# A planned two-layer kernel: one more resident value slice, smaller attention buffers, a new order and a new pacing of transfers

## Chip, cores and metric

The kernel runs on one core of one Trainium2 chip. The metric is the device time of one execution in microseconds (us); the times shown are the median of three runs.

## What is computed

The input x has 2048 tokens of 640 numbers in bfloat16. Two kinds of layer follow each other, twice each with the same weights: x = x + A(layernorm(x)), x = x + B(layernorm(x)).

Layer A is attention over segments of 32 tokens with a recurrent memory of 8 rows. It has 32 heads of 192. For each of 64 segments, in order:

```python
h = jnp.concatenate([mem, xs], axis=1)               # 40 rows
q, k, v = h @ Wq, h @ Wk, h @ Wv                     # 640 -> 32 heads x 192 each
p = softmax(where(mask, q @ k.T * scale, -1e9))
o = (p @ v) @ Wo                                     # 6144 -> 640
mem = o[:, :8, :]; outs.append(o[:, 8:, :])
```

The memory rows of a segment's output are the memory of the next segment, so the segments are a chain. Layer B is an MLP mixer: layer norm, a 640x640 matmul and a tanh-GELU, a shift of four feature groups by one or two tokens, a second 640x640 matmul, then a block 640 to 1536 to 640 with a GELU.

## The kernel before

Both attention layers run at once, in two lanes. Lane 1 is the second layer and runs LAG = 5 segments behind lane 0. `attention_step(t)` does segment t of lane 0 and segment t - 5 of lane 1 side by side, in the columns of one tile `hT`, so that one pass of the weights through TensorE serves both. There are 69 steps: 0 to 4 have only lane 0, 5 to 63 both, 64 to 68 only lane 1. With two lanes a matmul's moving operand has 80 columns (40 rows a lane), with one lane 56.

In a step the 32 heads are 8 groups of four (`HG = 4`), and two groups make a pair. For each of the four pairs, `keys_queries` projects keys and queries of a group (L940), `values3` (two lanes, L993) or `values` (one lane, L1028) the values of the pair, and `attend` does scores (`pss`, L1048), masked softmax on VectorE and ScalarE (L1060 to L1073, into the tile `Pm` or, in even two-lane steps, `Pm_e`), transposes (`pst`, L1082, copied into `PT` at L1090), the weighted values (`pso`, L1099) and their copy into an `oT` buffer (L1110, L1112). `project` multiplies oT by the output weights and accumulates all groups in `psy` (L1134). L1161 copies the new memory rows from `psy` into the next step's `hT`: nothing of the next step's projections can start before that. In even two-lane steps some value rows of the next step are computed ahead and put by in `stash`, and fetched back in the odd step (L1011).

`WO_FROM` says from which group on a projection may be held to the end of the step; it keeps its oT buffer until then, and `OT_BUFS` is their number. The MLP runs in chunks of 64 tokens a lane, one chunk for every two steps, from an even step on (`chunk`, `chunk_end`: psx, psl, psv2, psh, hs, y), between the attention's matmuls.

The attention weights are 31.5 MB [...]. `STREAM` says for each kind and pair how many of the five 128-row slices are loaded anew in every step; the other slices stay. A slice of a pair is 128x1536 bfloat16, 384 KB, and goes into one of 12 ring slots (`wst`, L817). Odd steps go through the pairs backwards, so that the pair at a turn is loaded once for two steps. The output weights are resident (L801). The MLP's weights pass through three slots (`wstB`, L853 to L859). All these loads are issued by SP in one order.

The order of all work is planned when the program is built. `Plan.add` records each operation with its engine, an estimate of its duration, what it reads and writes, a due time and a rank from the table `RANK`. `Plan.place` is a list scheduler: it always places the operation that can start first, and ranks decide among those that can start at nearly the same time. It models transfers with a rate (`DMA_RATE`, with one lane `RATE_ONE`). A load that would put more than 1 us of work ahead in the transfer model is delayed, and is "paced": in the program it waits for a matmul group, which the last lines of the kernel choose:

```python
elif o.paced:
    k = len(done) - 1
    while k >= 0 and done[k].end + PE_LAT > o.start:
        k -= 1
    if k >= 0:
        tc.add_manual_dep(o.last, done[k].last.name, dep, reason="pace")
```

Of the kernel before, what the change touches and what calls it, by code (L numbers as in the profile page):

```python
# [21 lines left out]
HG = 4  # L22
STREAM = {"k": (4, 2, 2, 4), "q": (4, 2, 2, 4), "v": (4, 1, 2, 4)}
# [8 lines left out]
WO_FROM = 3  # L32
# [9 lines left out]
OT_BUFS = 5  # L42
# [5 lines left out]
SWITCH = 0.095  # L48
LAT = 0.12
PE_LAT = 0.3  # L50
DMA_RATE = 350.0e3
# [9 lines left out]
RATE_ONE = 360.0e3  # L61
# [6 lines left out]
        "apply_ln.f": (29.559, 55.792, 17.416,),  # L68
        "chunk.f1": (23.781,),
        "chunk.f2": (55.346,),  # L70
        "chunk.f3": (49.334,),
        "chunk.fe": (36.823,),
        "chunk.fe3": (102.823,),
        "chunk.fel": (55.768,),
        "chunk.fh": (108.157,),
        "chunk.fhr": (14.733,),
        "chunk.fhs": (-1.703,),
        "chunk.fl": (17.93,),
        "chunk.fs": (3.514, 106.703,),
        "chunk.ft": (21.572,),  # L80
        "chunk.ftl": (23.993,),
        "chunk.fw": (19.421, 33.626, 37.652, 47.067, 46.903, 46.908, 51.102, 31.274, 56.07, 81.64, 83.785, 53.43,
            79.164,),
        "chunk.fx": (15.161,),
        "chunk.fx0": (112.491, 68.494,),
        "chunk.fxu": (105.007,),
        "chunk.fz": (124.455,),
        "gelu.f1": (41.515, 31.842, 65.448, 69.413, 29.704, 45.171, 6.969,),
        "gelu.f2": (19.582, 55.401, -1.038, -13.207, 27.337, 61.156, 95.68,),
        "gelu.f3": (36.826, 58.297, 18.949, 4.948, 30.821, 34.558, 18.885,),  # L90
        "gelu.f4": (55.18, 34.768, 63.375, -56.037, -0.096, 18.35, 22.907,),
        "ln_ops.f1": (3.817, 60.955,),
        "ln_ops.f2": (114.827, 95.473,),
        "load_b.fn": (42.665, 72.601, 73.122, 60.79, 46.44, 71.473, 46.173, 41.023, -13.973, -19.336, 68.295,
            43.387, 34.395,),
        "transposes.f": (18.738, 60.298, 22.802,),
    },
    "chunk_end": {
        "apply_ln.f": (40.67,),
        "chunk_end.fc": (62.442, 58.834, 83.754,),  # L100
        "chunk_end.fs": (36.579, 19.311,),
        "chunk_end.fst": (24.833, 137.421,),
        "chunk_end.fw": (77.354, 82.175, 46.044, 93.892, 86.198, 104.308,),
        "chunk_loads.f": (110.369, 92.579, 122.005, 106.334, 106.331,),
        "chunk_loads.fz": (111.9, -5.695,),
        "ln_ops.f1": (7.196,),
        "ln_ops.f2": (123.331,),
        "load_b.fn": (5.23, 1.719, 91.203, 49.097, 74.715, 52.663,),
        "transposes.f": (106.447,),
    },  # L110
    "first": {
        "attention_step.attend.f1": (68.897, 39.326, 41.804, 28.466, -8.574, 3.827, 12.182, 81.811,),
        "attention_step.attend.f2": (29.688, 3.725, 55.817, 85.348, 89.532, 54.11, 46.47, 42.088,),
        "attention_step.attend.f3": (37.804, 74.562, 24.632, 39.11, 84.711, 2.334, 12.184, 31.815,),
        "attention_step.attend.f4": (46.985, 133.184, 57.996, -14.888, 44.577, 61.056, 25.057, 28.659,),
        "attention_step.attend.f5": (72.24, 28.209, 80.373, 49.346, -18.442, -28.685, 28.798, 35.564,),
        "attention_step.attend.f6": (7.921, 29.359, -30.003, 43.173, 18.344, 41.846, 42.511, 55.051,),
        "attention_step.attend.f7": (13.361, 7.383, 43.256, 25.908, 20.236, 55.857, 75.302, -11.96, 21.812, -5.753,
            19.773, 72.6, 75.299, 95.674, 86.699, 88.497,),
        "attention_step.attend.fs": (46.721, 6.105, 1.413, -7.834, 21.699, 20.254, 21.569, 46.62,),  # L120
        "attention_step.fm": (55.427,),
        "attention_step.fy": (-0.204,),
        "attention_step.keys_queries.fk": (26.488, 18.209, 58.728, 7.772, 36.409, 64.332, -3.077, 23.72,),
        "attention_step.keys_queries.fk2": (-14.703, 2.672, 48.256, 53.233, 34.025, 40.988, 45.598, -2.059, 1.962,
            15.275, 34.847, -10.142, 39.767, 56.809, 63.46, 66.992,),
        "attention_step.keys_queries.fn": (21.571, 32.111, 16.117, -56.342, -41.907, 1.871, 54.408, 55.614, 11.212,
            18.753, 53.715, 66.651, 18.167, 23.251, 31.271, 32.948, 29.756, 7.549, 39.591, 50.473, -0.315, 18.167,
            48.365, 58.168, 44.747, 139.641, 21.246, 32.364, 22.87, 41.262, 64.464, 48.46, 83.925, 17.007, 19.065,
            16.202, 18.756, 33.666, 34.528, 40.661, 38.815, 44.173, 28.507, 19.545, 33.472, 24.726, 15.715, 51.317,
            45.935, 22.944, -5.271, 29.206, 49.555, 26.526, 25.7, 16.824, 43.548, 57.875, 33.742, 59.147, 64.063,  # L130
            27.622, 29.175, 81.7,),
        "attention_step.keys_queries.fq": (45.809, 18.135, 60.1, 65.753, 69.37, -1.427, 49.622, 44.462,),
        "attention_step.project.f8": (19.52, 33.909, -28.707, 107.592, 12.86, 77.771, 100.466, 23.989, 31.803,
            40.827, 40.837, 130.729, 36.057, 48.362, 41.26, 49.706,),
        "attention_step.v_copy.fe": (42.261, 47.784, 48.887, 71.528, 12.202, 49.386, 41.804, 50.823, 64.266,
            49.318, 20.738, 66.436, 42.958, 63.832, 23.717, 24.613,),
        "attention_step.values.fv": (-41.285, 32.943, 26.797, 50.039, 35.587, 16.299, 43.359, 44.868,),
        "load_pair.fn": (14.648, 53.698, 35.518, 22.343, -20.956, 37.306, 71.774, 39.237, 19.839, 12.575, 20.573,
            58.077, 54.069, 54.009, 75.338, 62.619, 8.153, -3.245, 80.829, 54.072, 43.384, 63.592, 35.638, 18.998,
            20.67, 44.7, 62.346, 9.067, 39.164, 19.703, 48.316, 36.251, 10.435, 5.137, 75.941,),  # L140
        "res_tile.fn": (73.432, 28.558, 56.529, 20.582, 69.248, 38.979, 29.597, 74.898, 15.641, 75.959, 55.693,
            44.577, 0.319, 29.095, 42.3, 49.248, 29.964, 107.836, 49.865, 17.493,),
    },
    "last": {
        "apply_ln.f": (-20.574, 76.742, 91.655,),
        "chunk.fc2": (45.814, 9.139,),
        "chunk.fhr": (-49.46,),
        "chunk.fs": (65.9, 36.918,),
        "chunk.ft": (54.865,),
        "chunk.fw": (48.117, 33.495, 45.73, 17.024, 46.488, 12.234, 41.248, 25.194, 32.675, 94.494, 70.8,),  # L150
        "chunk.fx": (25.434,),
        "chunk.fxu": (45.171,),
        "chunk.fz0": (78.323,),
        "chunk.halves.fa": (27.094, 106.57,),
        "chunk.halves.fd": (-49.02, 71.767,),
        "chunk.halves.fn": (77.02,),
        "gelu.f1": (17.472, 32.155, 99.763, 91.572, 38.995, 48.095,),
        "gelu.f2": (11.863, 37.133, 19.592, 31.791, 91.583, 13.808,),
        "gelu.f3": (38.816, 63.043, 83.342, 80.205, 21.478, 58.951,),
        "gelu.f4": (-10.272, 39.611, -4.107, 48.457, 78.558, 99.684,),  # L160
        "ln_ops.f1": (28.421, -18.981,),
        "ln_ops.f2": (44.289, 103.361,),
        "load_b.fn": (21.293, 70.515, 34.095, 6.385, 49.625, 62.984, 43.433, 10.52, 22.43, 49.618, 76.588, 9.262,
            76.276,),
        "transposes.f": (31.423, -1.2,),
        "warm.fwarm": (32.401, -16.818, 47.675, 21.047, 64.891, 28.29, 48.878, 42.379, 30.258, 92.789, 28.894,
            39.585, 19.172,),
    },
    "last_end": {
        "chunk_end.fs": (103.409, 12.202,),  # L170
        "chunk_end.fst": (53.517, 65.451, 1.877, 30.054,),
        "chunk_end.fw": (48.61, 122.515, 29.136, 50.074, 10.083, 12.93, 28.51, 21.247,),
        "load_b.fn": (11.244, 75.885, 68.713, 49.999, 55.019, 53.695,),
    },
    "start": {
        "apply_ln.f": (103.828,),
        "chunk_loads.f": (0.033, 14.73, 144.506,),
        "ln_ops.f1": (24.785,),
        "ln_ops.f2": (122.216,),
        "start.f1": (65.561,),  # L180
        "start.f2": (79.115,),
        "start.f3": (47.921,),
        "start.f4": (33.718,),
        "start.f5": (40.419, 48.193, 69.503, 117.792,),
        "transposes.f": (62.646,),
    },
    "step0": {
        "attention_step.attend.f1": (-11.22, 35.238, 17.075, 18.583, 70.388, 34.765, 47.388, 68.986,),
# [1571 lines left out]
```

## Time and profile before

| | |
|---|---|
| median of three runs | 3275.02 us (3273.39 to 3279.2) |
| the profiled execution, its own time | 3273.35 us |
| its span, first to last instruction | 3271.6 us |
| mean granted TensorE clock | 0.992 |
| moved by DMA | 860.41 MB, mean 263 GB/s |
| matmuls, and as many weight loads | 77341 |

In the profile, PE is TensorE's matmuls and PEld its weight loads, DVE is VectorE, ACT ScalarE, POOL GpSimd, and SP issues transfers. L940 is line 940 of the kernel before. A matmul's end is modelled: its recorded duration is some 0.2 us, while matmuls of 80 columns start 36 ns apart. "Idle before" an instruction is time after the modelled end of the one before it, with the releaser that ended the wait; "issue" means that no releaser is known. Numbers in waits are total us, times, and the longest in us.

### The profile page before, as it was taken

How to read it: one execution, taken by the hardware profiler on the slowest of the kernel's cores; microseconds unless marked ns; L12 is line 12 of the kernel's file. 1: busy time of each engine (PE TensorE's matmuls, PEld its weight loads, DVE VectorE, ACT ScalarE, POOL GpSimd, SP SyncE). 2: the span in 40 equal slices, each digit the busy share in tenths (PEclk: the TensorE clock that was granted, in tenths of full speed). 3: DMA queues.
4: the chain of work that ended last, by engine and by line, in shares of the span. 5: the costliest groups of instructions: out<-in, count | busy, mean ns of one | idle time of the engine just before them, and what ended most of it. 6: DMA issues, size and time to landing. Idle time of an engine off the chain costs nothing.

```text
span 3271.6 us, 173713 instructions
## 1 busy us (share of the span) xinstructions
PE 3154.7 (96%) x77341; PEld 2792.5 (85%) x77341; DVE 2314.6 (71%) x6857; ACT 1891.5 (58%) x4837; POOL 242.1 (7%) x485
## 2 busy tenths in 40 slices
PE   6899999999999999999999999999999999999987
PEld 4778888888888888888888888888888888888776
DVE  3566777777777777777777777777777777777665
ACT  2346566666565666665656666565656666656443
POOL 0000000000000000000000000000000000000000
PEclk7999999999999999999999999999999999999999
DMA  9887778777777877787778777877877787778786
GB/s 374 280 283 261 247 257 273 248 247 270 269 255 249 278 258 248 248 284 262 255 243 289 246 242 253 278 253 242 278 260 248 248 282 260 256 242 289 266 280 221
DMA packets 419560, 860.41 MB, mean 263 GB/s; under 512 B 40784, under 2 KB 208415, under 8 KB 418808
## 3 DMA queue, kind: packets, MB, share of 16 engines
q1 hardware_dynamic: 411512, 836.21, 74.6%
q8 instruction: 606, 9.93, 1.2%
q0 software_dynamic: 7136, 13.00, 1.2%
q14 instruction: 146, 1.20, 0.1%
q10 hardware_dynamic: 160, 0.08, 0.0%
HBM read 843.88 MB, written 5.24 MB: 260 GB/s over the span
## 4 chain that ended last, share of the span: by engine, by line
PE 90%; DMA 4%; DVE 2%; issue 2%; ACT 1%; SPq 0%; POOL 0%; POOLq 0%; ACTq 0%; DVEq 0%
PE psy L1134 17%; PE psq L940 17%; PE psk L940 17%; PE psv L993 15%; PE pss L1048 5%; PE pso L1099 4%; PE y L1599 3%; PE psh L1553 3%; PE pst L1082 2%; DMA wst<-in_A_Wq_dram 2%; PE psv L1028 2%; PE psh L1431 1%; PE hs L1490 1%; DMA wst<-in_A_Wk_dram 1%; PE psv L1204 1%
## 5 line engine op out<-in xcount | busy, mean ns | idle before, releaser
L940 PEld LDWEIGHTS <-wst 128*128 128x128 bf16 x19872 | 803.8, 99 | 64.4 <-issue 47.2
L1134 PE MATMUL psy<-oT,wo 128*128 128x80 bf16 (+1 forms) x16560 | 697.6, 200 | 24.9 <-issue 11.7
L973 ACT CAST V<-psv 96x384 bf16<-96x384 f32 (+4 forms) x1264 | 588.8, 473 | 213.1 <-PE psv L993 140.7
L1134 PEld LDWEIGHTS <-wo 128*128 128x128 bf16 x16560 | 628.0, 99 | 68.2 <-issue 53.8
L940 PE MATMUL psq<-hT,wst 128*128 128x80 bf16 (+1 forms) x9936 | 543.8, 200 | 25.6 <-DVE hT L1161 14.9
L940 PE MATMUL psk<-hT,wst 128*128 128x80 bf16 (+1 forms) x9936 | 533.9, 200 | 7.5 <-issue 4.6
L993 PEld LDWEIGHTS <-hT 128*32 128x32 bf16 (+1 forms) x11840 | 294.8, 96 | 162.5 <-issue 9.1
L948 ACT CAST qT<-psq 128x480 bf16<-128x480 f32 (+1 forms) x552 | 291.4, 528 | 136.8 <-PE psq L940 108.0
L993 PE MATMUL psv<-wst,hT 128*32 128x384 bf16 x6512 | 366.4, 326 | 0.0
L1060 DVE CUSTOM_DVE_ANT_1 pss<-pss,mask 80x320 f32<-80x320 f32 (+2 forms) x552 | 258.3, 468 | 127.8 <-PE pss L1048 84.0
L963 ACT CAST kT<-psk 64x160 bf16<-64x160 f32 (+1 forms) x552 | 152.0, 275 | 323.4 <-PE psk L940 134.0
L940 PE MATMUL psq<-hT,wq 128*128 128x80 bf16 (+1 forms) x6624 | 320.1, 200 | 7.2 <-issue 3.5
L940 PE MATMUL psk<-hT,wk 128*128 128x80 bf16 (+1 forms) x6624 | 321.4, 200 | 2.2 <-issue 1.2
L993 PE MATMUL psv<-wv,hT 128*32 128x384 bf16 x5328 | 321.6, 328 | 0.2 <-issue 0.2
L1110 ACT CAST oT<-pso 128x240 bf16<-128x240 f32 (+1 forms) x552 | 189.0, 342 | 227.2 <-PE pso L1099 172.4
L1112 DVE CAST oT<-pso 128x240 bf16<-128x240 f32 (+1 forms) x552 | 213.4, 387 | 127.4 <-ACT oT L1110 59.7
L963 DVE CAST kT<-psk 64x160 bf16<-64x160 f32 (+1 forms) x552 | 174.2, 316 | 181.6 <-ACT kT L963 129.2
L1090 ACT COPY PT<-pst 80x320 bf16<-80x320 bf16 (+2 forms) x552 | 220.9, 400 | 131.6 <-PE pst L1082 123.1
L956 DVE CAST kT<-psk 128x320 bf16<-128x320 f32 (+1 forms) x552 | 255.8, 463 | 45.0 <-ACT kT L963 31.4
L940 PEld LDWEIGHTS <-wk 128*128 128x128 bf16 x6624 | 268.1, 100 | 13.0 <-issue 12.7
L940 PEld LDWEIGHTS <-wq 128*128 128x128 bf16 x6624 | 266.2, 99 | 9.3 <-issue 5.5
L1048 PE MATMUL pss<-kT,qT 128*128 128x80 bf16 (+2 forms) x3312 | 242.8, 210 | 13.9 <-issue 3.8
(148 smaller groups left out, 4265.1 us busy)
## 6 DMA issues: line engine op xcount, KB each, us to landing
wst<-in_A_Wk_dram SPq DMA_DIRECT2D x556, 384.0 KB, 5.0
wst<-in_A_Wq_dram SPq DMA_DIRECT2D x556, 384.0 KB, 5.0
wst<-in_A_Wv_dram SPq DMA_DIRECT2D x487, 384.0 KB, 5.2
wstB<-in_B_w_dram SPq DMA_DIRECT2D x495, 320.0 KB, 4.8
wstB<-in_B_w_dram SPq DMA_DIRECT2D x132, 160.0 KB, 4.4
wo<-in_A_Wo_dram SPq DMA_DIRECT2D x8, 960.0 KB, 12.3
xw<-in_A_x_dram POOLq DMA_DIRECT2D x31, 80.0 KB, 4.8
x2d<-vbg POOLq DMA_DIRECT2D x31, 80.0 KB, 5.1
```

The costliest lines, as they stand in the source:

```text
L940: nc.tensor.matmul(out=o[:, cc, 0:W], lhsT=wv(kc, GW * j + cc * P, GW * j + (cc + 1) * P), rhs=h[:, kc, cw:cw + W], start=begin(pq), stop= ...
L948: nc.scalar.copy(out=qT[:, :, c0:c0 + N], in_=T(pq)[:, :, off:off + N])
L956: nc.vector.tensor_copy(out=k4[:, :, 0::3, c0:c0 + N], in_=p4[:, :, 0::2, off:off + N])
L963: copy(out=k4[r0:r1, :, jj, c0:c0 + N], in_=p4[r0:r1, :, 1, off:off + N])
L973: (nc.vector.tensor_copy if e == "DVE" else nc.scalar.copy)(out=v_part(*dst), in_=a_)
L993: nc.tensor.matmul(out=o[32 * u:32 * u + n3, :], lhsT=left[:, kc, 32 * g3:32 * g3 + n3], rhs=wv(kc, a, a + GWH), start=(kc == 0), stop=(kc ...
L1048: nc.tensor.matmul(out=o[0:m_, i * N:(i + w_) * N].rearrange("p (a b) -> p a b", a=w_), lhsT=qTw[:, c * NS:c * NS + m_], rhs=k_[:, j:j + w ...
L1060: nc.vector.tensor_tensor_reduce(out=o, in0=o, in1=maskt.unsqueeze(1).to_broadcast([NR, HG, N]), scale=-scale, scalar=3.0e38, op0=ALU.add, ...
L1090: nc.scalar.copy(out=Pt[0:KV, :, 0:N], in_=T(pst)[0:KV, :, c0:c0 + N])
L1110: nc.scalar.copy(out=o_[:, 3:6, off:off + N], in_=T(pso)[:, 3:6, 0:N])
L1112: nc.vector.tensor_copy(out=o_[:, 0:3, off:off + N], in_=T(pso)[:, 0:3, 0:N])
L1134: nc.tensor.matmul(out=o[:, m, cw:cw + W], lhsT=wo[:, cc, m * P:(m + 1) * P], rhs=o_[:, cc, 0:W], start=st, stop=True, skip_group_check=True)
```

## The change

One more of the five value slices of pair 2 stays on chip. Room for it, 3072 bytes in each partition, comes from three oT buffers instead of five, from one softmax tile `Pm` with the wider layout for all steps instead of two tiles, and from a `stash` without its gaps, whose copies are then two instructions in place of one. Projections of groups 3 and 4 are no longer held to the end. A load is tied to a matmul group that may end up to 0.25 us later than before; the planner's rates are lower and some of its estimates differ. Key and query projections get order edges (each starts after the first part of the one before; the second group of a pair with two lanes waits for the values of the pair before), one-lane values come after the scores planned before them and leave one PSUM slot free, and the whole table of ranks is another.

```diff
-STREAM = {"k": (4, 2, 2, 4), "q": (4, 2, 2, 4), "v": (4, 1, 2, 4)}
+STREAM = {"k": (4, 2, 2, 4), "q": (4, 2, 2, 4), "v": (4, 1, 1, 4)}
-WO_FROM = 3
+WO_FROM = 5
-OT_BUFS = 5
+OT_BUFS = 3
-SWITCH = 0.095
+SWITCH = 0.105
 LAT = 0.12
+PACE = 0.25
+OVER = 0.07
-DMA_RATE = 350.0e3
+DMA_RATE = 335.0e3
-RATE_ONE = 360.0e3
+RATE_ONE = 350.0e3
 RANK = {
...
-            free[e] = o.end
+            free[e] = o.end - (OVER if e in ("ACT", "DVE") else 0.0)
...
-    stash = ctile([P, 2, 2 * VP], bf16, "stash")
-    Pmw = ctile([NS, HG * NS], bf16, "Pm")
-    Pm = Pmw[:].rearrange("p (c n) -> p c n", c=HG)
-    Pm_e = ctile([NS, (HG - 1) * KR + P], bf16, "Pm_e")
+    stash = ctile([P, 2, 2, 2 * Dh], bf16, "stash")
+    Pmw = ctile([NS, (HG - 1) * KR + P], bf16, "Pm")
+    Pm = Pmw[:, 0:HG * KR].rearrange("p (c n) -> p c n", c=HG)[:, :, 16:KR]
...
+    last_v = []
+    seq_kq = []
...
-                    last_op[kind] = add("PE", mm_us(W, k=GC * len(kcs)), due + 0.01 * kcs[0], fn, r=(wb, *hk), a=(pq,))
+                    last_op[kind] = add("PE", mm_us(W, k=GC * len(kcs)), due + 0.01 * kcs[0], fn, r=(wb, *hk), a=(pq,),
+                                        order=(*(last_v[-2:-1] if j and both else ()), *seq_kq[-1:]))
+                    own_kq.append(last_op[kind])
+                seq_kq.append(own_kq[0])
...
                 def fst(op, j=j):
-                    st_, v_ = stash[32 * pr:32 * pr + 32, j, :], Vt[j][64:96, :] if behind_v else Vt[j][0:32, :]
-                    nc.vector.tensor_copy(out=v_ if behind_v else st_, in_=st_ if behind_v else v_)
+                    rows = Vt[j][64:96, :] if behind_v else Vt[j][0:32, :]
+                    for a in range(2):
+                        st_ = stash[32 * pr:32 * pr + 32, j, a, :].rearrange("n (h e) -> n h e", h=2)
+                        v_ = rows.rearrange("n (h x) -> n h x", h=2)[:, :, 256 * a:256 * a + Dh]
+                        nc.vector.tensor_copy(out=v_ if behind_v else st_, in_=st_ if behind_v else v_)
...
-                pv = ps("A", [P, GWH], f32, "psv")
+                pv = ps("A", [P, GWH], f32, "psv", 1)
...
-                add("PE", mm_us(GWH, k=KC), s0 + 0.05 * hf * sl, fv, r=(*wbs, *hk), w=(pv,), mode=64)
+                add("PE", mm_us(GWH, k=KC), s0 + 0.05 * hf * sl, fv, r=(*wbs, *hk), w=(pv,), mode=64, order=placed_before("pss"))
...
-            while k >= 0 and done[k].end + PE_LAT > o.start:
+            while k >= 0 and done[k].end + PE_LAT > o.start + PACE:
                 k -= 1
```

## Prediction before the run

> **What bounds the kernel now.** I read engine shares first, then the run cut into stages, then TensorE's waits by stage, then transfers. From the page:
>
> ```profile
> PE 3154.7 (96%) x77341; PEld 2792.5 (85%) x77341; DVE 2314.6 (71%) x6857; ACT 1891.5 (58%) x4837; POOL 242.1 (7%) x485
> ```
>
> TensorE is the bound; the question is only what idle time is left on it. Cut at the copies of the recurrent memory (step 0; steps 1 to 4 with one lane; steps 5 to 63 with two; steps 64 to 68 with one; the last MLP chunk), the table by stage is (columns: stretch, length, busy PE, PEld, DVE, ACT, POOL, clock, DMA share, GB/s):
>
> ```profile
> 88.90:254.53 165.63, 150.11 (x4029) 128.72 (x4029) 109.33 (x379) 71.62 (x231) 7.92 (x17) 0.99 0.80 273
> 254.53:3034.59 2780.06, 2746.16 (x67186) 2452.16 (x67184) 2031.34 (x5879) 1705.89 (x4249) 210.37 (x411) 1.00 0.76 259
> 3034.59:3243.00 208.41, 186.26 (x5023) 159.93 (x5023) 134.33 (x467) 89.03 (x283) 14.24 (x30) 0.99 0.82 284
> 0.00:88.90 88.90, 54.07 (x954) 41.37 (x955) 24.95 (x92) 17.41 (x55) 7.96 (x24) 0.74 1.00 368
> 3243.00:3271.60 28.60, 18.10 (x157) 10.30 (x154) 14.68 (x40) 7.52 (x21) 1.65 (x3) 0.99 0.34 113
> ```
>
> Step 0 is bound by DMA (share 1.00). The two-lane steps hold 85% of the time and TensorE idles 33.9 of 2780 us there; the one-lane stages idle 15.5 and 22.2 us. TensorE's waits in the two-lane stretch (us in total, times, longest):
>
> ```profile
> PE psq L940 <- DVE hT L1161: 14.9, 29, 0.5
> PE psq L940 <- issue: 4.4, 8, 1.1
> PE psy L1134 <- issue: 3.8, 7, 0.9
> ...
> PE psq L940 <- DMA wst<-in_A_Wq_dram: 1.4, 4, 0.4
> PE psk L940 <- DMA wst<-in_A_Wk_dram: 0.7, 3, 0.3
> ```
>
> Two things stand out. Once per two steps the first query projection waits for the copy of the recurrent memory: 29 waits of 0.51 us. The other wait is "issue", for nothing that the profile names. In the last one-lane stage it is longer:
>
> ```profile
> PE psy L1134 <- issue: 4.2, 3, 2.6
> PE psq L940 <- issue: 3.0, 2, 2.0
> ```
>
> I laid the starts of such stalls against the packets of the instruction queue:
>
> ```profile
> q8 instruction: 606, 9.93, 1.2%
> ```
>
> 606 packets of 16 KB are 256 instructions each, and 77341 loads plus 77341 matmuls over 256 is 604: this queue feeds TensorE. All 45 "issue" stalls above 0.1 us end 0.9 to 1.7 us after one of its packets ended; a random moment does so in 15% of cases. So TensorE runs out of instructions because a fetch came late. Just before those late fetches 3.1 weight transfers were in flight; over the two-lane stretch the mean is 2.1. A stall costs more than its gap, since a matmul's modelled end lies 0.2 us after its start and the next starts 36 ns after it; by start-to-start times the 45 cost 7.7 us (steps 1 to 4), 17.3 (two lanes) and 13.4 (steps 64 to 68), together **38.4 us**. Waits for weights cost about 3 us outside step 0.
>
> [...]
>
> **The change part by part.**
>
> *One value slice more stays on chip (STREAM v, pair 2: two streamed to one).* Each step loses one 384 KB transfer, except that step 0 loads it into its resident place: 68 fewer of
>
> ```profile
> wst<-in_A_Wv_dram SPq DMA_DIRECT2D x487, 384.0 KB, 5.2
> ```
>
> so about 419, and 26.7 MB less of 860 (3.1%). Transfers aren't the bound after step 0, so the saved bytes count only by what they unblock. Step 0 still loads every weight once: 0.
>
> *Pacing.* A paced load is tied to the last matmul group that ends 0.3 us ahead of its planned start; the change allows 0.25 us more, so loads leave up to 0.25 us later and nearer to plan. The planner's rate falls from 350 to 335 KB/us, so two loads in a row are planned 1.174 us apart and no longer 1.123; with one lane 1.123 for 1.092. Fewer bytes, wider spacing and less early issue all thin out what is in flight when a fetch comes. How much is that worth? Stall cost per time is 17.3/2780 = 0.6% at DMA share 0.76, 7.7/166 = 4.6% at 0.80 and 13.4/208 = 6.4% at 0.82. Read as a slope, taking 3% off the traffic (2.4 points of share) would remove over 60%; but with one lane the matmuls are also shorter, so a block of instructions is used up faster and part of the slope is that. I take half of 38.4: **-19 us**. Bounds: nothing gained, or 30 us.
>
> The opposite term: later loads. By landings and the waiting instruction on the same semaphore, 5% of the attention loads in the two-lane stretch land within 0.3 us of their use. The order is planned anew with these slower rates, so I take 0; bounds -3 (the waits for weights go) and +29 (worked out below). What queues behind a waiting load on SP is only other loads.
>
> *Smaller buffers.* oT from 5 to 3, with projections of groups 3 and 4 no longer held to the end of the step. The end of an odd step shows what is needed:
>
> ```profile
> 1333.56 0.46 PE L1099 MATMUL pso<-PT,V 80*128 80x80 bf16 x8
> 1333.85 2.86 PE L1134 MATMUL psy<-oT,wo 128*128 128x80 bf16 x75
> 1337.22 0.38 PE L940 MATMUL psq<-hT,wst 128*128 128x80 bf16 x6 [0.51 <-DVE hT L1161]
> ```
>
> After the last group's output only 75 projection matmuls remain, at 30 a group: two and a half groups, which three buffers hold. The old order hardly uses five: 0. In step 0 output weights come last, so groups 3 to 7 now wait in PSUM for them; the projections there idle 1 to 1.7 us for each output weight already: 0, at most +4.
>
> One P tile for two: the rows of the two layouts cost the same,
>
> ```profile
> L1067 ACT ACTIVATE Pm<-pss,sm 80x320 bf16<-80x320 f32 x208 | 108.7, 523 | 78.0 <-PE pst L1082 44.3 <-DVE sm L1060 32.7
> L1067 ACT ACTIVATE Pm_e<-pss,sm 80x320 bf16<-80x320 f32 x208 | 108.5, 522 | 13.4 <-DVE sm L1060 7.8
> ```
>
> and a step uses only one of them: 0. The stash copy becomes two of 2x192 in place of one of 896 elements:
>
> ```profile
> L1011 DVE COPY stash<-V x232: 373/380/389, 313.0 to 2985.6; 32x896 bf16<-32x896 bf16 x116
> L1011 DVE COPY V<-stash x232: 383/385/390, 348.7 to 3026.6; 32x896 bf16<-32x896 bf16 x116
> ```
>
> Proportional to elements, two take 0.33 us; if all fixed, 0.77. I take 0.5: 464 times 0.12 is 56 us more of VectorE work. [...] VectorE idles 749 us in the two-lane stretch and nothing is shown waiting for the stash: 0 on the path.
>
> *Order searched anew, new order edges.* The diff does not show the order that results. The same matmuls stay, and the best pair of steps takes 93.3 us, with the memory wait as its one hole. That wait costs 0.68 us start to start, 29 times: 19.7 us. It stands where an even step begins: its MLP chunk needs the output of the step just done, so it has nothing to offer. I take 0; bounds -20 (hole filled) and +20 (the other boundary, now covered by MLP matmuls, opens as wide). With one lane the softmax chain shows through (values, P, oT: some 12 us over nine steps): 0, bounds -5 and +5.
>
> **Sum.** -19 against the profiled execution's own 3273.35 us (span 3271.6 and 1.75 around it) gives 3254; the median of the runs shown is 3275.02, 1.7 above, so the forecast is **3256 us**.
>
> **Rivals.**
> 1. *Late weights: slower.* If planned use doesn't follow the later issue, loads that now land under 0.25 us ahead are late: 4.5% of some 2150 is 97, each costing 0.13 us and 0.17 of refilling: +29. With 19 regained: 3285. It decides from 63 late loads (19/0.3), one in 34. For: the margin is thin. Against: slower rates put planned landings later, and TensorE waits for loads only 8 times in the two-lane stretch.
> 2. *A second hole per pair: no change.* New order edges and three buffers leave the even-to-odd boundary uncovered: 29 x 0.68 = +20, total 3276. For: fewer projections to hold back. Against: that boundary is covered by MLP matmuls, which stay.
> 3. *Better order.* The hole is closed as well: -39, 3236. Nothing shows independent work at that place.
> 4. *Nothing of it.* Late fetches come from bursts that one load fewer doesn't change: 3270 to 3275.
>
> **Numbers.** What this kernel's measurement can tell from no change is about 0.2%, 6.5 us. Forecast case 0.52, rival 3 0.13 (both faster); rivals 2 and 4 0.13, of which 0.11 within 0.2% and the rest 0.01 on each side; rival 1 and larger holes 0.22. Faster 0.66, same 0.11, slower 0.23. The forecast case alone spans 3240 to 3268; the range reaches to rival 3 and rival 1: 3232 to 3288.
>
> **What would show it.** Right: Wv loads near 419; "issue" waits of TensorE well under the 30 us of now, most of the fall in the one-lane stages; two-lane DMA share near 0.74; the memory wait still 29 times; stash copies twice as many at some 0.25 us. Wrong: waits on wst above 10 us, a second regular wait at a step's start, or "issue" waits unchanged.

## Result and the profile after

The changed kernel is slower: 3313.47 us (median of four runs, 3308.97 to 3318.65) against 3277.11 us for the kernel before on the same chip, a ratio of 1.0111 (95% interval 1.009 to 1.0132). The forecast was 3256 us, with a range of 3232 to 3288.

The profiled execution took 3318.65 us with a span of 3316.5 us. Its page, and the row of the two-lane steps from its table by stage (columns as in the prediction):

```profile
PE 3183.1 (96%) x77339; PEld 2809.2 (85%) x77341; DVE 2329.5 (70%) x7320; ACT 1898.7 (57%) x4837; POOL 235.1 (7%) x483
...
q8 instruction: 605, 9.91, 1.2%
...
PE 71%; DVE 20%; DMA 3%; issue 3%; ACT 2%; SPq 0%; POOL 0%; ACTq 0%; DVEq 0%; POOLq 0%
...
wst<-in_A_Wv_dram SPq DMA_DIRECT2D x418, 384.0 KB, 4.8
```

```profile
256.05:3077.41 2821.36, 2768.74 (x67196) 2462.78 (x67194) 2047.39 (x6343) 1714.12 (x4248) 204.13 (x411) 1.00 0.75 247
```

The chain that ended last, before:

```profile
PE 90%; DMA 4%; DVE 2%; issue 2%; ACT 1%; SPq 0%; POOL 0%; POOLq 0%; ACTq 0%; DVEq 0%
```

The shares of busy time hardly move. The chain that ended last does: its share on VectorE is 20% where it was 2% before, and on TensorE 71% where it was 90%. By stage, 41.3 of the 44.9 us by which the span grew lie in the two-lane steps (2821.4 for 2780.1 us). TensorE's waits there (total us, times, longest):

```profile
PE pst L1094 <- DVE Pm L1084: 15.6, 54, 0.4
PE psk L943 <- DVE hT L1173: 14.9, 29, 0.5
PE psy L1146 <- DVE oT L1124: 6.8, 28, 0.2
...
PE psy L1146 <- issue: 0.9, 2, 0.6
```

The 29 memory waits are the same. New are the first and the third line: the transposes of P (L1094) wait for the normalised softmax, the output projection (L1146) for VectorE's half of oT. Counted over every stall above 0.1 us, from start to start as in the prediction, the stretch has 85 stalls on Pm (35.0 us) and 28 on oT (11.3 us), where before it had one. They are regular: the best pair of two-lane steps takes 95.32 us where it took 93.31. The late instruction fetches did fall as forecast, from 17.3 to 3.5 us in this stretch and from 38.4 to 18.5 us in all: 19 "issue" stalls above 0.1 us, each ending 1.2 to 1.6 us after one of the 605 packets of q8 ended (154680 matmuls and weight loads, so 255.7 a packet). So some 58 us of holes (2.01 us in each of 29 pairs) stand against some 15 us less of late fetches and late weights there. The stalls above 0.1 us account for 46 of the 58 us; the rest must lie in shorter ones, which were not counted.

### The profile page after: what moved, and what is told of

Same layout as the page of the kernel before. It is cut to its first block, busy times and chain, and to the rows that moved or that the text cites. A ratio compares the mean times of both kernels' runs of the same rounds, so it can differ in the third digit from the quotient of the medians.

```text
span 3316.5 us, 173787 instructions
## 1 busy us (share of the span) xinstructions
PE 3183.1 (96%) x77339; PEld 2809.2 (85%) x77341; DVE 2329.5 (70%) x7320; ACT 1898.7 (57%) x4837; POOL 235.1 (7%) x483
## 4 chain that ended last, share of the span: by engine, by line
PE 71%; DVE 20%; DMA 3%; issue 3%; ACT 2%; SPq 0%; POOL 0%; ACTq 0%; DVEq 0%; POOLq 0%
PE psy L1146 15%; PE psk L943 14%; PE psq L943 13%; PE psv L999 10%; PE pss L1059 3%; PE pso L1111 3%; PE y L1611 3%; PE pst L1094 3%; DVE Pm L1084 2%; DVE sm L1082 2%; DVE oT L1124 2%; PE psh L1565 2%; DVE kT L962 2%; DVE st L1192 2%; DVE pss L1071 2%
## 5 line engine op out<-in xcount | busy, mean ns | idle before, releaser
L1146 PE MATMUL psy<-oT,wo 128*128 128x80 bf16 (+1 forms) x16560 | 701.8, 200 | 33.3 <-DVE oT L1124 11.3
L1146 PEld LDWEIGHTS <-wo 128*128 128x128 bf16 x16560 | 631.6, 99 | 75.5 <-issue 63.6
L979 ACT CAST V<-psv 96x384 bf16<-96x384 f32 (+3 forms) x1264 | 583.1, 473 | 119.2 <-PE psv L999 54.5
L943 PE MATMUL psq<-hT,wst 128*128 128x80 bf16 (+1 forms) x9936 | 530.2, 200 | 4.9 <-DMA wst<-in_A_Wq_dram 3.8
L943 PE MATMUL psk<-hT,wst 128*128 128x80 bf16 (+1 forms) x9936 | 503.6, 200 | 18.4 <-DVE hT L1173 14.9
L1078 ACT ACTIVATE Pm<-pss,sm 80x320 bf16<-80x320 f32 (+2 forms) x552 | 277.7, 503 | 118.6 <-DVE sm L1071 102.1
L999 PE MATMUL psv<-wv,hT 128*32 128x384 bf16 (+1 forms) x5920 | 343.9, 328 | 0.0
L999 PE MATMUL psv<-wst,hT 128*32 128x384 bf16 x5920 | 341.8, 326 | 0.0
L969 ACT CAST kT<-psk 64x160 bf16<-64x160 f32 (+1 forms) x552 | 151.9, 275 | 314.9 <-PE pss L1059 170.8
L1082 DVE TENSOR_REDUCE sm<-Pm 80x4 f32<-80x320 bf16 (+2 forms) x552 | 250.5, 454 | 64.3 <-ACT Pm L1078 57.3
L969 DVE CAST kT<-psk 64x160 bf16<-64x160 f32 (+1 forms) x552 | 174.3, 316 | 158.5 <-ACT kT L969 89.9
L1071 DVE CUSTOM_DVE_ANT_1 pss<-pss,mask 80x320 f32<-80x320 f32 (+2 forms) x552 | 256.6, 465 | 34.5 <-PE pss L1059 26.1
```

The costliest lines, as they stand in the source:

```text
L943: nc.tensor.matmul(out=o[:, cc, 0:W], lhsT=wv(kc, GW * j + cc * P, GW * j + (cc + 1) * P), rhs=h[:, kc, cw:cw + W], start=begin(pq), stop= ...
L969: copy(out=k4[r0:r1, :, jj, c0:c0 + N], in_=p4[r0:r1, :, 1, off:off + N])
L979: (nc.vector.tensor_copy if e == "DVE" else nc.scalar.copy)(out=v_part(*dst), in_=a_)
L999: nc.tensor.matmul(out=o[32 * u:32 * u + n3, :], lhsT=left[:, kc, 32 * g3:32 * g3 + n3], rhs=wv(kc, a, a + GWH), start=(kc == 0), stop=(kc ...
L1071: nc.vector.tensor_tensor_reduce(out=o, in0=o, in1=maskt.unsqueeze(1).to_broadcast([NR, HG, N]), scale=-scale, scalar=3.0e38, op0=ALU.add, ...
L1078: nc.scalar.activation(out=Pb[0:NR, :, 0:N], in_=o, func=ACT.Exp, bias=sm_[0:NR, 0:1], scale=-1.0)
```

## Experiments

Most kernels here keep one order of work fixed: the list scheduler is replaced by one that takes operations in a stored order (read from the plan of before or of after), so that a constant can be changed and every queue stays as it was. In three_oT the queues move a little all the same: an operation that finds no oT buffer is passed by those behind it, and 31 of the operations of ScalarE and 31 of VectorE stand elsewhere. "Pair" is the shortest pair of two-lane steps, the last pair left out; "holes" are stalls on Pm, oT, PT, qT and kT, "fetch" late instruction fetches and "weights" stalls on weight loads, all above 0.1 us, from start to start, in the two-lane stretch, in us.

| kernel | time (ratio, interval) | pair | holes | fetch | weights |
|---|---|---|---|---|---|
| before | 3275.6 to 3279.2 | 93.31 | 0.3 | 17.3 | 4.2 |
| after | 3313.5 (1.0111, 1.009 to 1.0132) | 95.32 | 46 | 3.5 | 3.0 |
| tie_only | 3284.7 (1.0026, 1.0016 to 1.0035) | 93.31 | 0.4 | 18.9 | 7.0 |
| tie_rate | 3294.3 (1.0045, 1.0028 to 1.0062) | 93.56 | 0 | 19.7 | 24.5 |
| three_oT | 3384.2, a single run | 97.05 | 93 | 25.5 | 3.0 |
| after_old_pacing | 3321.6 (1.0125, 1.0109 to 1.0141) | 95.31 | 44 | 17.7 | 0 |
| pace_zero | 3313.1 (1.0105, 1.0082 to 1.0128) | 95.31 | 45 | 4.9 | 0 |
| no_slice_old_pacing | 3329.3 (1.0154, 1.0129 to 1.0179) | 95.31 | 46 | 16.5 | 0.7 |
| half_stash | 3299.4 (1.0064, 1.0043 to 1.0084) | 94.72 | 26 | 4.8 | 0.4 |
| swap_five | 3290.2 (1.0039, 1.0028 to 1.005) | 94.37 | 20 | 6.1 | 1.4 |
| swap_oT | 3351.2 (1.0224, 1.0199 to 1.0249) | 96.29 | 82 | 4.3 | 0.4 |
| new_order | 3493.8 (1.0657, 1.0641 to 1.0672) | 100.81 | 176 | 28.6 | 2.5 |
| new_order_old_pacing | 3479.2 (1.0609, 1.0591 to 1.0628) | 100.82 | 181 | 12.4 | 0 |
| ruled_new | 3300.3 (1.0063, 1.0045 to 1.0081) | 93.41 | 0 | 58.3 | 3.4 |
| ruled_old | 3309.8 (1.0105, 1.0079 to 1.013) | 93.71 | 1 | 59.6 | 4.1 |
| spaced_new | 3255.3 (0.9941, 0.9922 to 0.996) | 92.77 | 0 | 23.9 | 2.8 |
| spaced_old | 3282.6 (1.002, 1.0008 to 1.0032) | 93.23 | 1 | 30.7 | 9.3 |

### The pacing and the buffers alone, on the order of before

tie_only:

```diff
-while k >= 0 and done[k].end + PE_LAT > o.start:
+while k >= 0 and done[k].end + PE_LAT > o.start + PACE:      # PACE = 0.25
```

> The kernel before with PACE = 0.25 alone: the planned order, rates and buffers are those of before, only the matmul group to which a paced load is tied may end 0.25 us later. Theory 1 (the new order itself has holes; pacing helps): a pair of two-lane steps keeps its floor of 93.3 us, late instruction fetches fall from 38 us to 20 to 30, and the time is 3260 to 3270 against 3277. Theory 2 (later loads are what slows the changed kernel): TensorE's waits on wst rise well above 3 us outside step 0 and the time goes over 3290.

tie_rate, the same with the new rates on the stored order of before:

```diff
-DMA_RATE = 350.0e3
+DMA_RATE = 335.0e3
-RATE_ONE = 360.0e3
+RATE_ONE = 350.0e3
```

> The order of before, replayed operation by operation, with PACE = 0.25 and the planner's transfer rates of the change (335 and 350 KB/us). Slices and buffers as before. Theory 1: floor of a pair still 93.3 us, late fetches lower than with the tie alone (10 to 20 us in all), time 3255 to 3268. Theory 2: waits for weights of 20 us or more and a time over 3290.

three_oT, the stored order of before:

```diff
-OT_BUFS = 5
+OT_BUFS = 3
```

> The order of before, replayed, with three oT buffers in place of five and nothing else changed; an operation that finds no buffer waits and the ones behind it go ahead. My prediction had it that the old order hardly uses five: then it stays at 3270 to 3285. Theory 1: the old order holds projections of up to five groups as filler through the step, three buffers push softmax outputs back, and a pair takes 2 to 5 us more: 3340 to 3430.

Measured: on the order of before, neither the tie alone nor the tie with the new rates lowers the late fetches (18.9 and 19.7 us for 17.3), and both times lie above what theory 1 expected. With the rates the weights are late, 24.5 us, as theory 2 had it for this kernel. That is the prediction's first rival in small. The buffers that were costed at nothing cost 107 us, in a single run; its pair, 3.7 us longer, says the same. TensorE's waits in the two-lane stretch of three_oT, and one of ScalarE's:

```profile
PE psy L834 <- ACT oT L810: 27.2, 58, 0.5
PE pst L782 <- DVE Pm L773: 19.4, 29, 1.0
...
PE pss L748 <- ACT qT L648: 11.2, 29, 0.7
```

```profile
ACT oT L810 <- PE psy L834: 77.9, 29, 2.9
```

In the old order, some groups' oT keeps its buffer for some 20 us, because their projection is held back as filler. With three buffers a copy into oT waits for such a projection once per pair (the last line), and what is queued behind the copies on ScalarE and VectorE (qT, the softmax) is late with it. So the change had to be planned anew, and what holes it has are those of the new order.

### Pacing and slice, on the order of after

after_old_pacing (rates 350 and 360, no tie), pace_zero (new rates, no tie) and no_slice_old_pacing (old pacing, and the slice streamed again):

```diff
-PACE = 0.25
+PACE = 0.0
-DMA_RATE = 335.0e3                                           # not in pace_zero
+DMA_RATE = 350.0e3
-STREAM = {..., "v": (4, 1, 1, 4)}                            # no_slice_old_pacing only
+STREAM = {..., "v": (4, 1, 2, 4)}
```

> The changed kernel with its own order, replayed, and the pacing of before (PACE = 0, rates 350 and 360). Theory 1: the holes of the new order stay (a pair of two-lane steps at 95.3 us), late fetches return by some 10 to 15 us: 3320 to 3330. Theory 2: without the later ties the time goes back to 3270 to 3285.

> The changed kernel with the same order and the new rates (335 and 350), but each paced load is tied to the last matmul group that ends 0.3 us before its planned start, without the 0.25 us more: loads leave a little earlier. Theory 1 (the 0.25 us tie is what took away the late fetches, 21 stalls and 17.7 us under the old pacing against 6 and 3.5 us): fetch stalls in the two-lane stretch rise to 12 us or more and the time by 5 to 9 us, to 3318 to 3323. Theory 2 (the lower rate, which spaces the loads wider, did it): fetch stalls stay at 3 to 7 us and the time within 3 us of 3313.5.

> The order of the changed kernel with the old pacing (as after_old_pacing: no 0.25 us tie, rates 350 and 360), and the extra value slice of pair 2 streamed again in every step, beside the one that already is: 69 more transfers of 384 KB (487 in place of 418 for Wv). Theory 1 (one slice less of traffic is what thins out the late instruction fetches): fetch stalls in the two-lane stretch rise above those 17.7 us of after_old_pacing, to 22 or more, waits for weights appear, and the time is 5 to 15 us above its 3321.6. Theory 2 (the slice is beside the point as long as transfers are no bound): fetch stalls 16 to 20 us, time within 4 us of 3321.6. The holes at pst and psy stay in both.

Measured: the holes stay with the order whatever the pacing (44 to 46 us, pair 95.31). The late fetches follow the rate, not the tie: 17.7 us with the old rates, 4.9 with the new ones and no tie, 3.5 with both. The slice doesn't touch them in this stretch (16.5 against 17.7). Streaming it again took 7.7 us more, which is in theory 1's range of time, but the intervals of the two ratios overlap. In the two profiled executions half of the difference lies in steps 1 to 4 (172.8 us for 168.3), but pace_zero, which doesn't stream the slice, takes 174.1 us there; so a price of the slice is not shown. Why the same rates did nothing on the order of before is not settled.

### Why the new order has holes

half_stash leaves out the second of the two stash copies, and with it half of the stashed values:

```diff
-                    for a in range(2):
+                    for a in range(1):
```

> The changed kernel with its order of work, rates and pacing kept instruction for instruction, but only the first of the two stash copies is made each time (the second half of the stashed values is left out, so VectorE is relieved of 232 copies of 0.21 us). Theory 1 (VectorE runs a few hundredths of a microsecond per operation behind the plan in which the order was found, so every wait of the transposes for the softmax product, Pm, grows out of VectorE's queue): the pair of two-lane steps falls from 95.6 us by 0.7 to 1.1, the waits of pst for Pm fall from 20.3 us to under 10, the time falls by 20 to 32 us, to 3281 to 3294. Theory 2 (the holes come from order edges or from PSUM and oT buffers coming free late, VectorE being only the last named): at most 5 us are gained and the waits on Pm stay at 18 to 21 us.

The trace has 464 copies fewer, two for each of the 232 that the expectation counts. 14 us gained, less than theory 1 said and more than theory 2: VectorE's lateness is part of the cause, but its load is not all of it. Of the stalls, those on oT vanish (11.3 to 0.3 us) and those on Pm fall from 35.0 to 25.9 us.

new_order then tried an order found by shifting operations in a model of the plan with a slower VectorE (`OVER` is how much too early the plan takes ScalarE and VectorE to be free after an operation):

```diff
-OVER = 0.07                                                  # order of the changed kernel
+OVER = 0.02                                                  # another stored order
```

> All of the change is kept (the value slice on chip, three oT buffers, one P tile, two stash copies, order edges, rates and tie), but the order of work is another: starting from the order of the changed kernel, operations were shifted by small amounts in a model of the plan in which VectorE and ScalarE come free 0.05 us later per operation (OVER 0.02 in place of 0.07), with a second, slower setting counted in. Planned pair of steps 92.70 us, and 93.0 with OVER 0; the changed kernel's order has 92.68 in its own plan but 97.7 with OVER 0. Theory 1 (the order, found in a plan that is too kind to VectorE, makes the holes; three buffers and the slice do not): measured pair 93.2 to 93.9, waits of pst on Pm and of psy on oT under 3 us together in the two-lane stretch, fetch stalls there 3 to 10 us, time 3262 to 3278, at or below the kernel before. Theory 2 (with three oT buffers and the two-part stash copies the holes come back wherever the order puts them): pair 94.5 or more, time 3290 or more.

> As new_order, with the old pacing: rates 350 and 360, no 0.25 us tie. Planned pair 92.70 as well. Theory 1 (wider spacing of loads takes away late fetches wherever the order leaves room for it): fetch stalls in the two-lane stretch 12 us or more above those of new_order, the time 5 to 15 us above it. Theory 2 (the fall of late fetches belonged to the order of the changed kernel alone, where loads wait behind holes): stalls as in new_order within 4 us, time within 4 us.

In new_order theory 1 missed by far: the pair took 100.8 us where the model had 92.7. The bounds of theory 2 hold, but not its reason: ruled_new and spaced_new below have the same three buffers and two-part copies, and no such holes. In new_order_old_pacing both theories missed: the old pacing took off 16 us of late fetches, the reverse of the order of after; why is open. The first miss showed what the model, and the planner, lack. ScalarE's waits in the two-lane stretch of new_order:

```profile
ACT oT L828 <- DVE oT L830: 269.4, 207, 2.6
...
ACT kT L675 <- DVE kT L675: 164.8, 144, 2.9
```

The two halves of oT read different columns of one PSUM tile and write different columns of one oT buffer; so do the three parts of kT. `Plan.add` knows no wait between them, because a read depends only on writers. Yet ScalarE waits for VectorE's half here, and VectorE for ScalarE's in the kernels before and after (for oT 34.5 and 120.1 us, below). In the traces the two take turns: none of the 552 pairs of oT halves overlaps in time, before or after. The program carries the wait in the order in which the copies are recorded (swap_five and swap_oT, below); whether anything in the chip asks for it is not shown.

The wait goes with the PSUM tile that is read, and not with the buffer that is written. In one-lane steps VectorE and ScalarE copy the two halves of a V tile out of two PSUM tiles, and in the trace of after 35 such pairs of copies into one V tile do overlap; one of them is in these merged lines:

```profile
94.71 1.12 DVE L979 CAST V<-psv 40x384 bf16<-40x384 f32 x2 [5.16 <-PE psv L1039]
...
95.52 0.96 ACT L979 CAST V<-psv 40x384 bf16<-40x384 f32 x2 [1.54 <-PE psv L1039]
```

The wait also stands between copies that share no partition, as two of the three kT copies:

```python
for part, (r0, r1, jj) in enumerate(((0, 64, 1), (64, P, 2))):      # ScalarE, then VectorE
    ...
    copy(out=k4[r0:r1, :, jj, c0:c0 + N], in_=p4[r0:r1, :, 1, off:off + N])
```

ScalarE's copy has partitions 0 to 63 and VectorE's second 64 to 127, and still none of the 552 copies of kT on ScalarE overlaps one on VectorE, before or after. Whether these two have to take turns is not shown; no run here tries them without the wait.

VectorE's waits in the two-lane stretch, before and then after:

```profile
DVE kT L963 <- ACT kT L963: 108.6, 89, 2.7
DVE oT L1112 <- ACT oT L1110: 34.5, 70, 1.6
DVE kT L956 <- ACT kT L963: 20.4, 62, 0.9
```

```profile
DVE oT L1124 <- ACT oT L1122: 120.1, 63, 4.0
...
DVE kT L962 <- ACT kT L969: 75.9, 87, 1.4
DVE kT L969 <- ACT kT L969: 65.4, 118, 2.4
```

That is 164 us before and 261 after; 108.6 and 65.4 us of it (VectorE's L963 before, L969 after) are between the two kT copies that share no partition. Not all of it is this wait's own: ScalarE's half of oT had itself waited for the matmul in all 70 of the waits for it before and in 61 of the 63 after, and counted from its start on, 24.8 of the 34.5 us and 24.4 of the 120.1 are left. But all of it stands at the head of VectorE's queue. The copies of the recurrent memory out of psy wait in the same way, 103.1 us before and 88.7 after, and are left out here, as that did not grow. One hole of after, in the timeline (start, duration, instruction, idle before and releaser; other lines left out), shows how it gets to TensorE:

```profile
1240.21 0.49 DVE L962 CAST kT<-psk 128x320 bf16<-128x320 f32 x1 [1.13 <-PE pss L1059]
...
1240.81 0.28 ACT L969 CAST kT<-psk 64x160 bf16<-64x160 f32 x1 [0.33 <-PE psq L943]
...
1241.13 0.33 DVE L969 CAST kT<-psk 64x160 bf16<-64x160 f32 x1 [0.43 <-ACT kT L969]
1241.48 0.49 DVE L1071 CUSTOM_DVE_ANT_1 pss<-pss,mask 80x320 f32<-80x320 f32 x1
...
1242.11 0.52 ACT L1078 ACTIVATE Pm<-pss,sm 80x320 bf16<-80x320 f32 x1 [0.56 <-DVE sm L1071]
...
1243.82 0.47 DVE L1082 TENSOR_REDUCE sm<-Pm 80x4 f32<-80x320 bf16 x1
...
1244.54 0.49 DVE L1084 TENSOR_TENSOR Pm<-Pm,sm 80x320 bf16<-80x320 bf16 x1
...
1245.08 0.32 PE L1094 MATMUL pst<-ident,Pm 80*128 80x80 bf16 x4 [0.42 <-DVE Pm L1084]
```

The three kT copies run one after the other. ScalarE's starts 0.11 us after the end of VectorE's first (the profile names psq as its releaser, which ended within 0.03 us of that copy), and VectorE's second 0.04 us after the end of ScalarE's; these last two are the ones that share no partition. VectorE stands still for 0.43 us; the softmax behind it starts that much later; VectorE is then busy, with gaps of at most 0.05 us, to the product Pm; and TensorE waits 0.42 us at the transposes.

The test is to keep every engine's queue and to turn only the wait round. swap_five and swap_oT do that (the operations exchanged are neighbours, with no other work of at least one of the two engines between them). As a sketch, since the edit itself is another stored order:

```diff
 ...                         # recording order of one pair of copies
-ACT  oT[:, 3:6] <- pso[:, 3:6]
 DVE  oT[:, 0:3] <- pso[:, 0:3]
+ACT  oT[:, 3:6] <- pso[:, 3:6]
```

> The changed kernel with every engine's own queue in exactly the same order; only the order in which two copies out of one PSUM tile are recorded is exchanged, at five places per pair of steps (147 in all: one or two halves of oT and three parts of kT). The copies of one PSUM tile made by ScalarE and by VectorE run one after the other in the order of recording, which the plan doesn't know; exchanged, ScalarE's copy waits for VectorE's at these five places and no longer the other way round. Theory 1 (VectorE stands at the head of its queue waiting for ScalarE's half, and the softmax chain behind it comes late: that makes the holes at pst and psy): with this rule added to a model of the plan, and delays fitted so that the pairs of before, after, half_stash, three_oT and new_order come out within 0.3 us, the pair of steps is 94.3 in place of 95.2, so here some 94.4 measured after 95.3, and the time falls by 20 to 30 us, to 3283 to 3294. Theory 2 (VectorE is late by its own load, and who waits for whom among copies is beside the point): pair 95.1 to 95.5, time within 5 us of 3313.5.

> The changed kernel with every engine's own queue in exactly the same order; for 291 of the 552 oT pairs, those where nothing of either engine's work lies between, VectorE's half is recorded before ScalarE's, so that ScalarE waits for VectorE. Theory 1 (the two copies of one PSUM tile run one after the other in the order recorded): the model with that rule gives a pair of 96.6 in place of 95.2, so 96.4 to 97.0 measured, waits ACT oT <- DVE oT take the place of many DVE oT <- ACT oT, time 3345 to 3375. Theory 2 (no such rule decides): pair and time as in the changed kernel, 95.3 and 3313 within 5 us.

Both came out as theory 1 had them: 3290.2 us with 147 pairs exchanged where it helps, 3351.2 with 291 of the 552 oT pairs exchanged, pairs of 94.37 and 96.29 (the latter just under the 96.4 expected), from the same instructions in the same queues. TensorE's waits, swap_five and then swap_oT:

```profile
PE psy L845 <- DVE oT L823: 6.2, 26, 0.2
PE pst L793 <- DVE Pm L783: 3.4, 22, 0.2
```

```profile
PE psy L845 <- ACT oT L821: 28.8, 30, 1.3
PE pst L793 <- DVE Pm L783: 18.8, 78, 0.4
```

In swap_five the waits on Pm fall from 15.6 to 3.4 us. In swap_oT they do not fall, and the projection now waits for ScalarE's half, which waits for VectorE's. So the wait is shown as a cause. It is not all: swap_five wins back 23 of the 36 us that the change lost, and how the rest divides among other places of the wait and VectorE's own load (half_stash) was not separated.

### Structure or order

ruled_new and ruled_old shift the orders of after and of before in the model with the wait in it (copies of one PSUM tile take turns):

> All of the change is kept (slice on chip, three oT buffers, two-part stash copies, order edges, tie and rates); the order of work is another, found by shifting operations in the model that knows the rule (ScalarE's and VectorE's copies out of one PSUM tile run one after the other in the order recorded). Modelled pair of steps 92.8 us (before 93.4, changed kernel 95.2). Theory 1 (the loss of the changed kernel is its order, made by a plan without that rule; three buffers and the slice allow an order at least as tight as the old one): measured pair 92.8 to 93.2, waits of pst on Pm and of psy on oT under 3 us together in the two-lane stretch, fetch stalls there under 12 us, time 3238 to 3262, below the kernel before. Theory 2 (three buffers and the longer stash copies themselves keep the structure behind the old one): pair 93.8 or more, time 3280 or more.

> The kernel before (five oT buffers, two P tiles, no slice more, old rates, no tie), with its order of work shifted in the same model in the same way, from its own order as the start. Modelled pair 92.9 us in place of 93.4. Theory 1 (order alone is what separates kernels here, and the old structure gains only what was left in it): pair 92.9 to 93.3, late fetches as before (15 to 20 us in the two-lane stretch), time 3248 to 3268, so 5 to 15 us above ruled_new, the difference being the late fetches. Theory 2 (the old order is already at what the old structure allows): pair 93.3, time 3270 to 3278.

The holes are gone in both, the best pair is within 0.6 and 0.8 us of the model's, and neither is faster: late fetches took their place, 58.3 and 59.6 us. So theory 1 was right about the holes and missed the time. TensorE's waits in ruled_new:

```profile
PE psq L650 <- issue: 20.0, 26, 2.6
PE psk L650 <- issue: 14.9, 18, 1.9
```

A likely cause lay at hand. A paced load is tied to a matmul group recorded ahead of it, and in these stored orders loads were recorded early: the tie was 1.42 us ahead of the planned start on average, and one load in six had the same tie as the one before. Of the loads, 16% were issued within 0.5 us of the one before (before 2.8%, after 0.2%). spaced_new and spaced_old record each load later, with every queue as it was (again a sketch):

```diff
 ...                         # recording order; PE, ACT, DVE, POOL and SP queues unchanged
-SP  wst <- Wk               # recorded early, tied to a group long past
 PE  psq ...
 PE  psy ...
+SP  wst <- Wk               # tied to the group nearest to its planned start
```

> ruled_new with every engine's queue in exactly the same order; only the place at which each load is recorded is later, so that it is tied to the matmul group nearest to its planned start (0.30 us ahead of it on average, as in the changed kernel with 0.28) and not to one long before it (1.42 us ahead in ruled_new, where 16% of the loads were issued within 0.5 us of the one before and 69 late instruction fetches in the two-lane stretch cost 58.3 us). Theory 1 (loads that leave in bunches hold up the instruction fetches): loads within 0.5 us of the one before under 1%, late fetches in the two-lane stretch cost 3 to 20 us, time 3240 to 3266, below the kernel before. Theory 2 (late fetches come from TensorE running without holes, whatever the loads do): 45 us or more stay, time 3290 or more.

> ruled_old in the same way: every engine's queue in the same order, loads tied 0.58 us ahead of their planned start on average (kernel before 0.54, ruled_old 1.05). Theory 1 (bunched loads hold up instruction fetches): late fetches in the two-lane stretch fall from 59.6 us to about those of the kernel before, 12 to 25 us, time 3255 to 3280, 5 to 20 us above spaced_new. Theory 2 (late fetches come from TensorE running without holes): 45 us or more stay, time 3295 or more.

spaced_new takes 3255.3 us, a ratio of 0.9941 (0.9922 to 0.996): it beats the kernel before by 20 us and the changed kernel by 58, with all of the change but its order. Loads within 0.5 us of the one before fall to 5.8%, late fetches to 23.9 us; theory 1 had expected under 1% and at most 20 us. That the place of the loads cost ruled_new some 34 us of late fetches is shown. That it was their bunching is not: the loads also left later, and in new_order_old_pacing, with 16.2% in bunches, late fetches cost only 12.4 us. The row of the two-lane steps from spaced_new's table by stage, and TensorE's waits there:

```profile
251.20:3020.90 2769.70, 2733.06 (x67186) 2451.27 (x67184) 2052.21 (x6343) 1678.79 (x4248) 206.84 (x411) 1.00 0.75 252
```

```profile
PE psk L650 <- DVE hT L880: 14.4, 28, 0.5
PE psk L650 <- issue: 4.2, 5, 1.5
```

No stall above 0.1 us on Pm or oT is left, and the best pair, 92.77 us, is below that of before. spaced_old misses its range by 2.6 us at 3282.6, slower than the kernel before, from whose order its own was shifted: step 0 takes 94.7 us for 88.9, and late fetches and weights are 30.7 and 9.3 us. So three buffers, two-part stash copies and the slice have no loss of their own that an order could not avoid; how much of the 27 us between the two is structure and how much the luck of a search is open.

## Why the prediction was wrong, point by point

- **Late fetches, -19:** right in size, in good part by luck. In all they fell by 19.9 us (38.4 to 18.5), but the reasons were half wrong. The slope over the stages said that most would go with one lane; it went in the two-lane steps (17.3 to 3.5), while steps 64 to the end kept 12.4 of 13.4. The slice and the tie did nothing for it there, the rate did, and only with this order. That weights in flight hold up a fetch was an estimate from 3.1 transfers against 2.1; how the one does it to the other is not shown. Nor is it shown that a block of instructions is used up faster with one lane: the projections' matmuls start 26 ns apart there and 36 with two lanes (medians, before), but by the table by stage TensorE takes 24.3 matmuls a us in steps 1 to 4 and 24.2 in the two-lane steps.
- **Late weights, 0:** right in the changed kernel (3.0 us for 4.2). On the order of before the same settings cost 20 us of late weights (tie_rate), so "planned anew" was needed for this 0.
- **Slice:** Wv loads 418 for 419 forecast, DMA share 0.75 for 0.74.
- **oT buffers, 0:** failed. "Two and a half groups, which three buffers hold; the old order hardly uses five" was read from the end of one step. The buffers are used in the middle of it, where a group's projection is held as filler. On the old order three buffers cost 107 us.
- **Stash, 0 on the path:** the extra work was put too high (two copies of some 245 ns take 0.42 us together where 0.5 was taken, an estimate between 0.33 and 0.77, and VectorE's busy time in two-lane steps rose from 2031.3 to 2047.4 us, by 16 and not by 56), and the 0 was too low. "Nothing is shown waiting for the stash" held for the order of before. In the new one VectorE works almost without a gap ahead of the product Pm (at most 0.05 us in the hole shown above), and half of the copies is worth 14 us.
- **Order, 0 with bounds of 20 either way:** the step that failed and decided it. The best pair of 93.3 us was taken for a property of the matmuls; it was one of an order in which VectorE has room. The bound of +20 priced one new hole per pair at a step's end, as long as the memory wait. Measured were 2.01 us per pair, in some four holes inside the steps, so 58 us. The cause, as far as it is shown, is a wait that the planner doesn't know: in this program copies of two engines out of one PSUM tile exclude each other (no overlap in 552 pairs of oT halves), and turning it round at 147 places gains 23 us. VectorE's load adds to it. The wait was in the page of before, as VectorE's idle time behind ScalarE's kT and oT, and I read only TensorE's waits.
- **Rivals:** the second came nearest (a second hole per pair, from three buffers and new edges), but with the wrong place and a third of the price; the new edges do not force the holes, since ruled_new keeps them. Of the signs of being right, all came true but one (the late fetches fell in the two-lane steps and not with one lane), and of the signs of being wrong none did: there was none for a regular wait inside a step, so the list could not have told.

## What to carry to other kernels

When a change brings a new order of work, the waits that the planner leaves out can cost more than the change gains: look at the engines that feed the bound for idle time that is ended by another feeder, and try which way round it costs less. In this program two engines that copy out of one PSUM tile take turns (552 pairs of oT halves without an overlap), in the order in which the copies are recorded, so that order is a choice to be made like the queues themselves: turned at 147 places it was worth 23 us. And a buffer count is judged by how long the longest-held buffer lives over the whole period (some 20 us on the order of before, where three buffers cost 107 us), not at the point where the work ends.

## What the runs showed of the hardware

- In this program, copies out of one PSUM tile on ScalarE and VectorE take turns, at different columns and at different partitions alike: no overlap among 552 pairs of oT halves, nor among the copies of kT, in before and after. A copy that waited over 0.1 us starts some 0.03 us after the end of the other (medians in after: 33 ns for oT in both directions and for kT from ScalarE to VectorE, 88 ns for kT the other way). Only the turn of that wait, in unchanged queues, moved the time from 3313.5 to 3290.2 or to 3351.2 us.
- When TensorE's instruction fetches come late depends on when the loads leave: in the same queues, with loads tied 0.30 us ahead of their planned start on average and no longer 1.42, 69 stalls and 58.3 us in the two-lane stretch became 33 and 23.9 us. The share of loads within 0.5 us of the one before fell from 16% to 5.8% with it, but does not settle the loss alone: 12.4 us with 16.2% (new_order_old_pacing), 18.9 us with 0.1% (tie_only).
- A copy of 32 x 384 bf16 elements in SBUF takes VectorE some 245 ns, one of 32 x 896 took 380. Taken as a fixed part and a part per element, an estimate from these two alone, the fixed part is some 144 ns, most of the short copy.
